# The last two kinds of sums of w_out's blocks issued on GpSimd instead of VectorE, in a kernel of cosine-weighted linear attention and a leaky-ReLU layer

## Chip, cores and metric

The kernel runs on one core of a Trainium2 chip. The metric is the device time of one execution in microseconds; of several executions the median is given. The time before is 271.71 us, the median of three runs (271.64 to 272.72). Beside these one execution was profiled: it took 272.88 us, and the span of its trace, from the first to the last instruction, is 271.0 us.

## The reference

Attention without a softmax over 8 batches, 8 heads, 576 positions and 64 columns per head, and behind it a layer of 512 to 2048 to 512 over the 4608 tokens:

```python
def phi(x, c, s):                      # c, s: cos and sin of pi/2 * position / 576
    r = np.maximum(x, 0.0)
    return np.concatenate([r * c, r * s], axis=-1)
q_p, k_p = phi(q, cos_w, sin_w), phi(k, cos_w, sin_w)
kv = np.einsum('bhsf,bhsd->bhfd', k_p, v)
z = np.sum(k_p, axis=2)
num = np.einsum('bhsf,bhfd->bhsd', q_p, kv)
den = np.einsum('bhsf,bhf->bhs', q_p, z)[..., None] + 1e-06
x = (num / den), heads side by side     # (4608, 512)
h = x @ w_in                            # w_in: 512 x 2048
out = np.maximum(0.01 * h, h) @ w_out   # w_out: 2048 x 512
```

## The kernel before

**Tiles and stages.** The tokens go through in nine groups of 512: groups 0 to 7 are the first 512 positions of each batch, group 8 the 64 last positions of all batches. For each batch the kernel makes `kpm` and `kpt` (phi of k, `k_part`, L268, through `phi_half`, L240 on VectorE and L238 on ScalarE), casts v into `vmain` and `vtail`, multiplies them (`kv_mm`, L291 and L298) and copies the result out as `kv`. For each group it makes `qp` (phi of q), transposes it, multiplies by `kv` (`num`, L375, or in the first two groups `num_half`, L411) and divides (`divide`: `den` L386, `rden` L390, `xs` or `xp` L391, all on VectorE). The quotient is transposed into `xT`, and the two products of the layer follow.

**The two products.** Group 0 uses plain products (`ffn1`, L454; `ffn2`, L470). From group 1 on in the second product, and from group 2 on in the first, a product of 2 x 2 blocks is made with seven block products instead of eight (`p1`, L777; `p2`, L882). This needs sums of the blocks of each operand. The blocks of w_out lie in `w2` (16 chunks of 128 rows, 512 columns): b11 and b12 are the left and right halves of chunks 0 to 7, b21 and b22 those of chunks 8 to 15. `w2_sums(i, s)` makes the sum of kind s for half i of the chunks (chunks 4i to 4i+3 and 8+4i to 11+4i), each one instruction of 128 x 1024 elements in fp16:

- kind 1: `wb1` = b12 - b11
- kind 2: `wb2` = b22 - `wb1`
- kind 4: `wb4` = b21 - `wb2`
- kind 3: b12 = b22 - b12, written over b12 in `w2`

The block product 7 (of `p2`) reads the new b12, the block product 4 reads `wb4`; both come late in the order 1, 2, 6, 5, 7, 4, 3 of `f2_stream`. The plain product of group 0 reads the old b12.

**What sets the order.** All instructions are recorded by hand in one order, and each engine works through its own in that order; an instruction waits by semaphores for what it reads and for earlier readers of what it overwrites. The first part (groups 0 and 1 up to their quotients) is written out line by line, with small lists of steps woven between matmuls. The rest is a list of pairs of a position and a function (`put`), sorted by position and recorded at the end. A group takes 56 or 58 positions. The sums of w_out stand in two places:

- in the woven list of L668: kinds 1 of both halves, kinds 2 and 4 of the first half (`for i, n in ((0, 1), (1, 1), (0, 2), (0, 4)): at(9, w2_sums, i, n)`);
- in the position list, from the table `W2_AT` (L1051, loop L1077): kind 2 of the second half at 16.0, kind 3 of the first half at 29.5 and of the second at 18.5, kind 4 of the second half at 75.5. A table entry with one position serves the second half alone.

All of them are made by VectorE through `sub` (L254), which most other sums of blocks go through too (`gs`, `xw`, `wa`).

**GpSimd** (`POOL` in the code) has ten small setup instructions, and then eleven casts (L248): parts of w_in (`cast_w1`) and of v (`v_main(b, lo, hi, POOL)`, L570, L571 and L678). The last of these, for the second four heads of batch 1, is recorded right behind the four pairs `k_main(1, j, ACT, DVE, 4, 8)` (L677), whose cosine parts are ScalarE's and whose sine parts are VectorE's; `kv_half(1, 1, "n")` (L688) multiplies these.

Of the kernel before, what the change touches and what calls it, by code (L numbers as in the profile page):

```python
# [11 lines left out]
ALU = mybir.AluOpType  # L12
# [6 lines left out]
def kernel(  # L19
# [14 lines left out]
    nc = tc.nc  # L34
# [45 lines left out]
    ACT, DVE, POOL = nc.scalar, nc.vector, nc.gpsimd  # L80
# [169 lines left out]
    def add(o, a, b):  # L250
        nc.vector.tensor_tensor(out=o, in0=a, in1=b, op=ALU.add)  # L251

    def sub(o, a, b):
        nc.vector.tensor_tensor(out=o, in0=a, in1=b, op=ALU.subtract)  # L254

    def kp_tiles(b):
        st["kpm", b] = kppool.tile([P, H, J, F], dt.float16, name="kpm")
# [259 lines left out]

    wb = {s: const.tile([P, NH, N2], dt.float16, name=f"wb{s}") for s in (1, 2, 4)}

    def w2_sums(i, s):  # L520
        lo, hi = slice(4 * i, 4 * i + 4), slice(8 + 4 * i, 12 + 4 * i)
        left, right = slice(0, N2), slice(N2, DM)
        b11, b12 = w2[:, lo, left], w2[:, lo, right]
        b21, b22 = w2[:, hi, left], w2[:, hi, right]
        if s == 1:
            sub(wb[1][:, lo], b12, b11)
        elif s == 2:
            sub(wb[2][:, lo], b22, wb[1][:, lo])
        elif s == 4:
            sub(wb[4][:, lo], b21, wb[2][:, lo])  # L530
        else:
            sub(b12, b22, b12)

    def w1_sums(i, s, lo=0, hi=4):
        a11, a12, a21, a22, s1, s2, s4 = (
# [132 lines left out]
    for i, n in ((0, 1), (1, 1), (0, 2), (0, 4)):  # L668
        at(9, w2_sums, i, n)
# [340 lines left out]
    def put(pos, f, *args):  # L1010
        line.append((pos, len(line), f, args))
# [64 lines left out]
        put(top[ALL - 1] + at_, w1_sums, 1, s, 2, 4)  # L1076
    for s, at_ in W2_AT.items():  # L1077
        for i in range(2 - len(at_), 2):
            put(at_[i - 2], w2_sums, i, s)
    for s, at_ in G1_AT.items():  # L1080
        for u in range(2):
            put(at_[u], g_sums, 1, s, 4 * u, 4 * u + 4)
# [6 lines left out]
    for b in range(2, NG):  # L1089
        at_, eng, s0 = AT[min(b, 5)], ENG[min(b, 5)], top[b] if b > 3 else 0  # L1090
# [53 lines left out]
```

## Time and profile before

| | |
|---|---|
| median of three runs | 271.71 us |
| the profiled execution | 272.88 us |
| its span | 271.0 us |
| mean granted TensorE clock | 0.999 |
| VectorE, all subtractions of L254 of 128x1024 fp16, one instruction | 0.68 us |
| GpSimd, last instruction but for the end of the program | 45.75 to 46.79 us |

The engines are PE (TensorE), PEld (its weight loads), DVE (VectorE), ACT (ScalarE), POOL (GpSimd) and SP (SyncE, which issues the DMAs). The first part of the page gives each engine's busy time, its share of the span and its instructions. The part headed by the chain gives the work that ended last, followed back from the last instruction, in shares of the span. A timeline row has the start in us from the start of the span, the duration in us, the engine, the line of the kernel, the operation, the tile written, an arrow and the tiles read, the shape and the count of merged instructions; in brackets stands how long the engine sat idle before it and what ended that. A row of the chain has start, length and what ran.

### The profile page before, as it was taken

To read this page: it belongs to the slowest core of one execution; us is meant where nothing else is said; L and a number is where in the kernel's file an instruction comes from. 1 tells how busy PE (TensorE), PEld (TensorE's weight loads), DVE (VectorE), ACT (ScalarE), POOL (GpSimd) and SP (SyncE) were. 2 spreads that over 40 slices of the span, in tenths; PEclk is the share of its full clock that TensorE was granted. 3 is DMA by queue.
4 is the path that set the end of the run, shared out by engine and by line. 5 is a ranking of instruction groups with operands and counts; after the bars stand their busy time and mean duration, and the time that the engine had idled before them with its cause. 6 is when DMAs were issued, how large, how long until landed. Compare 5 with 4: busy or idle time off the path is not lost.

```text
span 271.0 us, 6597 instructions
## 1 busy us (share of the span) xinstructions
PE 263.2 (97%) x2660; PEld 226.1 (83%) x2660; DVE 201.6 (74%) x445; ACT 200.8 (74%) x330; POOL 10.6 (4%) x21
## 2 busy tenths in 40 slices
PE   7799999999999999999999999999999999999994
PEld 5786455765888989889999999999999889999983
DVE  5774799797986797899779696979577758644652
ACT  6666556696878998798899789978966756766621
POOL 1055101000000000000000000000000000000000
PEclk9999999999999999999999999999999999999999
DMA  6999999998999869998999699969384412200324
GB/s 229 313 355 409 408 350 371 354 241 269 296 225 350 148 189 259 297 189 238 280 261 158 184 273 271 175 208 157 77 135 160 62 41 95 82 0 2 144 50 119
DMA packets 87150, 57.05 MB, mean 211 GB/s; under 512 B 56656, under 2 KB 82256, under 8 KB 86608
## 3 DMA queue, kind: packets, MB, share of 16 engines
q1 hardware_dynamic: 86816, 56.37, 78.8%
q8 instruction: 21, 0.34, 0.5%
q10 hardware_dynamic: 304, 0.26, 0.3%
q14 instruction: 9, 0.07, 0.1%
HBM read 36.70 MB, written 9.44 MB: 170 GB/s over the span
## 4 chain that ended last, share of the span: by engine, by line
PE 89%; DVE 4%; DMA 3%; ACT 3%; issue 1%; SPq 0%; DVEq 0%; ACTq 0%
PE ps_o L882 33%; PE ps_h L777 29%; PE ps_h L454 5%; PE ps_h L490 5%; PE ps_o L470 5%; PE ps_h L882 3%; PE ps_num L375 3%; DMA kst<-in_k_dram 3%; PE ps_kv L291 2%; ACT g L751 1%; DVE kpm L240 1%; DVE xp L391 1%; PE ps_qt L365 1%; PE ps_kvh L291 1%; PE ps_numh L411 1%
## 5 line engine op out<-in xcount | busy, mean ns | idle before, releaser
L882 PEld LDWEIGHTS <-g 128*128 128x128 f16 x640 | 62.5, 98 | 7.3 <-DVE g L251 0.2
L251 DVE TENSOR_TENSOR u<-ps_h,u 128x512 f32<-128x512 f32 x52 | 35.8, 688 | 25.2 <-PE ps_h L777 22.3
L882 PE MATMUL ps_o<-w,g 128*128 128x256 f16 x352 | 51.2, 273 | 0.0
L777 PEld LDWEIGHTS <-w 128*128 128x128 f16 x416 | 44.4, 114 | 1.2
L777 PE MATMUL ps_h<-xT,w 128*128 128x256 f16 x288 | 43.3, 273 | 0.0
L804 ACT ACTIVATE g<-u 128x1024 f16<-128x1024 f32 x26 | 27.5, 1057 | 10.9 <-DVE u L251 10.8
L777 PEld LDWEIGHTS <-wa 128*128 128x128 f16 x312 | 34.0, 113 | 1.7 <-DVE xw L254 0.6
L790 ACT ACTIVATE g<-ps_h 128x512 f16<-128x512 f32 x52 | 31.2, 602 | 5.7 <-PE ps_h L777 5.7
L797 ACT COPY u<-ps_h 128x512 f32<-128x512 f32 x52 | 30.4, 585 | 5.5 <-PE ps_h L777 5.4
L882 PE MATMUL ps_o<-wb,g 128*128 128x256 f16 x232 | 33.5, 273 | 0.0
L777 PE MATMUL ps_h<-xw,wa 128*128 128x256 f16 x208 | 31.3, 273 | 0.3 <-DVE xw L254 0.3
L882 PEld LDWEIGHTS <-gs 128*128 128x128 f16 x256 | 24.9, 98 | 2.9
L900 ACT COPY ob<-ps_o 128x512 f32<-128x512 f32 (+1 forms) x32 | 17.9, 561 | 9.2 <-PE ps_o L882 9.0
L490 PE MATMUL ps_h<-xT,w 128*128 128x512 f16 (+1 forms) x104 | 24.7, 363 | 0.0
L391 DVE TENSOR_TENSOR xs<-ps_num,rden 128x512 f16<-128x512 f32 x28 | 19.3, 691 | 1.0
L882 PE MATMUL ps_o<-w,gs 128*128 128x256 f16 x120 | 17.8, 273 | 0.0
L251 DVE TENSOR_TENSOR ob<-ps_o,ob 128x512 f32<-128x512 f32 (+1 forms) x22 | 14.8, 674 | 3.7 <-ACT ob L900 1.4
L254 DVE TENSOR_TENSOR gs<-g 128x1024 f16<-128x1024 f16 x16 | 11.0, 688 | 8.8 <-ACT g L804 8.7
L882 PE MATMUL ps_o<-wb,gs 128*128 128x256 f16 x120 | 17.5, 273 | 0.0
L787 ACT COPY ps_h<-ps_h 128x512 f32<-128x512 f32 x26 | 14.9, 572 | 2.3 <-PE ps_h L777 1.5
L777 PE MATMUL ps_h<-xT,wa 128*128 128x256 f16 x104 | 15.6, 273 | 0.0
L777 PE MATMUL ps_h<-xw,w 128*128 128x256 f16 x104 | 15.6, 273 | 0.0
(112 smaller groups left out, 412.3 us busy)
## 6 DMA issues: line engine op xcount, KB each, us to landing
qst<-in_q_dram SPq DMA_DIRECT2D x7, 1024.0 KB, 6.3
out_dram<-ob SPq DMA_DIRECT2D x14, 512.0 KB, 2.8
kst<-in_k_dram SPq DMA_DIRECT2D x6, 1024.0 KB, 8.0
vst<-in_v_dram SPq DMA_DIRECT2D x6, 1024.0 KB, 7.5
w1st<-in_moe_w_in_dram SPq DMA_DIRECT2D x8, 512.0 KB, 9.9
w2st<-in_moe_w_out_dram SPq DMA_DIRECT2D x4, 1024.0 KB, 13.4
kst<-in_k_dram SPq DMA_DIRECT2D x4, 512.0 KB, 7.5
vst<-in_v_dram SPq DMA_DIRECT2D x4, 512.0 KB, 7.9
```

What stands on the lines that cost most here:

```text
L251: nc.vector.tensor_tensor(out=o, in0=a, in1=b, op=ALU.add)
L391: nc.vector.tensor_tensor(out=xs, in0=ps[:, :, 0 : 4 * NE].rearrange("p a (b e) -> p a b e", e=NE)[:, :, :, 0:D], in1=rden.rearrange("p (a ...
L454: nc.tensor.matmul(ps[:, m % 2, lo:hi], lhsT=w1[m // 4][c // 2][:, c % 2, m % 4 : 512 : 4], rhs=xT[:, c, lo:hi], start=(c == 0 and lo == 0 ...
L470: nc.tensor.matmul(ps, lhsT=st["g", g][:, m, tt * P : (tt + 1) * P], rhs=w2[:, m, :], start=(m == 0), stop=(m == NFT - 1),)
L490: nc.tensor.matmul(ps[:, lo:hi], lhsT=w1[m // 4][c // 2][:, c % 2, m % 4 : 512 : 4], rhs=st["xT", g][:, c, lo:hi], start=(c == 0 and lo == 0),
L777: nc.tensor.matmul(bank[:, p], lhsT=w(c), rhs=st["xb", g][n][:, c], start=(fresh and p == 0 and c == 0), stop=(c == 1), skip_group_check=True,
L787: nc.scalar.copy(bank1[bj], bank1[bi])
L790: nc.scalar.activation(st["g" + nm, g][:, 2 * t : 2 * t + 2], bank1[bi], AF.Lrelu)
L797: nc.scalar.copy(st["u", g, t][:, n], bank1[bi])
L804: nc.scalar.activation(st["gt", g][:, :, 1, 2 * t : 2 * t + 2], st["u", g, t], AF.Lrelu)
L882: nc.tensor.matmul(bank, lhsT=st[G2[n], g][:, m, pair * P : (pair + 1) * P], rhs=W2[n](m), start=(fresh and m == 0), stop=(m == NH - 1), s ...
L900: nc.scalar.copy(o_at(g, half_, col, pair), bank_of(bi, pair, pair is None))
```

## The change

`sub` and `w2_sums` get an engine as their last argument, VectorE unless another is given. Kinds 3 and 4 hand it on. The loop over the position table gives GpSimd for kinds above 2. The woven list gives none.

```diff
-    def sub(o, a, b):
-        nc.vector.tensor_tensor(out=o, in0=a, in1=b, op=ALU.subtract)
+    def sub(o, a, b, eng=DVE):
+        eng.tensor_tensor(out=o, in0=a, in1=b, op=ALU.subtract)
...
-    def w2_sums(i, s):
+    def w2_sums(i, s, eng=DVE):
...
         elif s == 4:
-            sub(wb[4][:, lo], b21, wb[2][:, lo])
+            sub(wb[4][:, lo], b21, wb[2][:, lo], eng)
         else:
-            sub(b12, b22, b12)
+            sub(b12, b22, b12, eng)
...
     for s, at_ in W2_AT.items():
         for i in range(2 - len(at_), 2):
-            put(at_[i - 2], w2_sums, i, s)
+            put(at_[i - 2], w2_sums, i, s, POOL if s > 2 else DVE)
```

In the built program GpSimd has three instructions more and VectorE three fewer; the order on TensorE, ScalarE and SyncE is as before.

## The prediction

> **What bounds the kernel now.** I read the busy shares first, then the chain of waits around the places of the moved work, then the timelines of GpSimd (POOL) and VectorE (DVE) there.
>
> ```profile
> PE 263.2 (97%) x2660; PEld 226.1 (83%) x2660; DVE 201.6 (74%) x445; ACT 200.8 (74%) x330; POOL 10.6 (4%) x21
> ...
> PE 89%; DVE 4%; DMA 3%; ACT 3%; issue 1%; SPq 0%; DVEq 0%; ACTq 0%
> ```
>
> TensorE is busy 97% of the span and is 89% of the chain that ends last. So freed VectorE time is worth something only where TensorE waits for VectorE, and any new wait of TensorE is paid in full, since there is almost no idle time later to earn it back in.
>
> The chain (start, length, what) where GpSimd finishes its last work of before:
>
> ```profile
> 47.92 0.45 PE ps_x L428 x8
> 48.37 0.35 PE ps_kvh L291 x8
> 48.72 0.06 PE ps_kvh L298
> 48.77 0.26 PE ps_kvh L291 x8
> ...
> 50.68 0.70 DVE xp L391
> 51.38 0.05 issue
> 51.43 0.40 PE ps_xth L428 x4
> ```
>
> The second group of eight L291 matmuls takes 0.26 us, the first 0.35. The first is paced by its weights, the four `kpm` sine parts that VectorE makes just then. The chain runs on through the sums of L411, the division (L391) and the transposes (L428): all of this is serial.
>
> VectorE and GpSimd there (start, duration, operation, idle before):
>
> ```profile
> 45.75 1.04 POOL L248 CAST vmain<-vst 128x1024 f16<-128x1024 f32 x1 [17.72 <-DMA vst<-in_v_dram]
> ```
>
> ```profile
> 46.59 0.69 DVE L391 TENSOR_TENSOR xp<-ps_numh,rden 128x512 f16<-128x512 f32 x1
> 47.20 1.13 DVE L240 TENSOR_SCALAR kpm<-kst,sin_t 128x256 f16<-128x256 f32 x4
> 48.25 0.68 DVE L248 COPY osb<-ps_o 128x512 f32<-128x512 f32 x1
> ```
>
> The last `kpm` part ends at 47.20 + 1.13 = 48.33, just when TensorE wants it. GpSimd is free from 45.75 + 1.04 = 46.79 to the end.
>
> **The change, part by part.** *What moves.* Three instructions, not four: the position table has kind 3 for both halves (29.5 and 18.5) and kind 4 for the second half only (75.5). Kind 4 of the first half comes from the earlier list (L668), which passes no engine, and stays on VectorE. VectorE loses the two `w<-w` and the last `wb<-w,wb`; GpSimd gets the same three behind its `vmain` cast. No DMA and no matmul moves, and no queue but these two changes its order.
>
> *What VectorE gains.* Each is 0.68 us long and 0.60 from its start to the next one's:
>
> ```profile
> 60.87 0.68 DVE L254 TENSOR_TENSOR w<-w 128x1024 f16<-128x1024 f16 x1
> 61.62 0.17 DVE L386 TENSOR_SCALAR den<-ps_num 128x8 f32<-128x8 f32 x1
> ...
> 88.41 0.17 DVE L386 TENSOR_SCALAR den<-ps_num 128x8 f32<-128x8 f32 x1 [0.48 <-PE ps_num L375]
> ```
>
> That is 3 x 0.60 = 1.8 us of VectorE, but none on the path. The one at 60.87 stands before a `den` at 61.62 that needs the matmuls of L375, and these end at 61.59 in the chain. The one at 68.64 lies in a queue that next goes idle at 79.67 (0.68 us idle, waiting for ScalarE) with TensorE busy throughout. The one at 85.62 is followed by 0.48 us of waiting for TensorE at 88.41. I cost the gain at 0; the most it could be is the 0.45 us that TensorE waits for `xs` at 62.89 and the 0.28 us for `xw` at 97.6, together 0.7.
>
> *When GpSimd starts.* "The same places" holds for the order of recording only. GpSimd does nothing between, so each instruction starts when its own inputs are there. In the built order the first `w<-w` (second half) waits for the casts of w_out (VectorE's ends at 44.70, ScalarE's at 45.32) and for the L470 matmuls that read these rows (over by 43.2, when the first L291 matmuls of this batch stand behind them); the next one has no wait at all. So both start not at 60.87 and 68.64 but back to back at 46.8, right behind the `vmain` cast and across the four `kpm` parts. Kind 4 needs the `wb` of kind 2 (59.66 to 60.34) and starts behind that. Readers are far off: the first product with the new `w` is at 77.47, that with the second half of the last `wb` at 88.65. So no reader waits.
>
> *What GpSimd takes (T each).* No row shows it subtracting. Its casts take 0.61 us for 512 elements and 1.04 for 1024, 0.84 ns for each further element with one input. Lower bound: as the cast, 1.04. Upper: a whole cast for each of the two inputs, 2.08. I take the upper, 2.1, since its row rate per input is the nearest thing; twice 1.04 would be too much only if the two inputs came in at once.
>
> *What it does to VectorE.* One place shows the two engines at once:
>
> ```profile
> 24.99 0.69 DVE L251 TENSOR_TENSOR wa<-w,w 128x1024 f16<-128x1024 f16 x1 [3.15 <-POOL w L248]
> 25.72 1.41 DVE L254 TENSOR_TENSOR wa<-wa,w 128x1024 f16<-128x1024 f16 x1
> 27.16 1.41 DVE L254 TENSOR_TENSOR wa<-w,wa 128x1024 f16<-128x1024 f16 x1
> ```
>
> ```profile
> 25.26 2.77 POOL L248 CAST w<-w1st 128x1024 f16<-128x1024 f32 x2 [0.30 <-DMA w1st<-in_moe_w_in_dram]
> ...
> 26.57 1.46 POOL L248 CAST w<-w1st 128x1024 f16<-128x1024 f32 x1
> ```
>
> Alone the sum takes 0.69 and the cast 1.04; here 1.41 and 1.31 to 1.46. The ends fit strict turns: cast 1 lets go at 26.57, the sum ends 0.56 later (27.13); cast 2 then needs 0.90 more (28.03), the next sum ends 0.54 after that (28.57). Each waits for a whole instruction of the other. Not everything waits: the division `xp` at 46.59, whose large input comes from PSUM, takes its usual 0.69 beside the cast of 45.75, and so does the one at 14.73 beside a cast.
>
> The four `kpm` parts read and write SBUF, with one tensor as input. No row shows such an operation beside GpSimd. Their rate (343 ns at 256 elements, 478 at 512: 0.53 ns each) is that of the sums from SBUF (418 at 512, 682 at 1024: 0.52) and twice that of the sums out of PSUM (422 at 256, 688 at 512: 1.04). So they are nearer to what waits than to what doesn't, and I take it that they wait their turn. Bounds: no effect (0), or full turns. By turns: the first subtraction holds from 46.80 to 48.90; the first `kpm` part ends 0.22 later (its 0.34 less the 0.12 that the blocked sum had done beforehand), the second subtraction follows from about 48.98 to 51.08, the second part ends at 51.30, the third and fourth 0.26 apart at 51.83. That is 51.83 - 48.33 = **3.5 us** late (2T - 0.7). TensorE stands for it at the first L291 group, and all behind it goes late by as much: the copy of `kv`, L411, the division, ScalarE's xT copies and the g evictions queued behind these. The loads into the stage buffers that these parts free go late by as much too.
>
> The Trainium skill, page "SBUF — State Buffer", section "Who interferes with whom", says that GpSimd and VectorE share one pair of ports under an exclusive lock, held for a whole instruction, and that copies, casts and tensor_scalar in a two-port mode fall under it as well as operations with two SBUF inputs; by this rule the sum is the 3.5 us above, and were only the second kind blocked, 0. The turns at 25 us agree for two inputs; no run here shows the other yet. The same skill's "GPSIMD Engine Reference", section 3.1, has 4497 ns for a two-input add of 2048 fp32 elements; half of it, 2.25 us, would be an estimate for T and make the sum 3.8 us, 275.5 in all.
>
> *Kind 4.* When it becomes ready `gs2<-g,gs3` (60.26, two SBUF inputs) is already under way, so GpSimd waits, and then VectorE has three divisions out of PSUM until 66.4. I cost it at 0; if it came first it would hold the `gs2` sum up by T, 2.1, of which the slot of 0.60 given free at 60.87 takes a part: at most 1.5.
>
> *Sum.* 0 + 3.5 + 0. The profiled execution took 272.88 us with a span of 271.0, so 1.9 lies around the span; its span would become 274.5 and its time 276.4. The median of the runs shown is 271.71, 1.17 below that execution, so I forecast 271.71 + 3.5 = **275.2 us**.
>
> **The rivals.**
> 1. *TensorE's clock falls in the stall.* At the end of this trace the granted clock is 1.00 until 270.0 and 0.50 from 270.5, some 2.9 us after the last matmul (267.4). The stall is 3.5 us, with one matmul or two of 65 columns in it. Against: 1.5 us without matmuls at 11 us left the clock at 1.00, and the longest piece here is about 2.1. If it falls, some 3 us of matmuls go at half speed, of which the stretch from 52.9 to 58.8 hides a part (36 matmuls of 0.11 us in 6 us): +1.3, so 276.5. The Trainium skill, "TensorE: Matmul & The Clock Gate", Part 1, gives an idle window of 3413 ns that runs freely of the kernel; the 2.9 us here is in accord.
> 2. *VectorE keeps its turn over all four parts*, as they are issued 0.26 apart without a wait between them (the two sums at 25 us have one). Then only one subtraction is in the way: 46.80 + 2.1 + 0.22 + 3 x 0.26 = 49.9, 1.6 late: 273.3.
> 3. *No wait for one-input operations* (not slower). If the `kpm` parts run beside GpSimd as the division does, nothing on the path is touched, the whole change is hidden and VectorE has 1.8 us more: 271.7, at best 0.7 less, 271.0. It decides by the `kpm` rows: if they still last 0.34 each, this is it.
> 4. *The change moves nothing* is excluded: the built order has the three on GpSimd.
>
> **How the numbers follow.** Full turns with the clock kept 0.52 (T 0.3 us to either side gives 2.9 to 4.1: 274.6 to 275.8), with the clock lost 0.18 (276.5, up to 277.2), one turn 0.16 (273.3), no wait 0.14. The last splits into no change 0.10 and faster 0.04. A difference under 0.5% (1.4 us) can't be told from none here; one turn gives 1.6, so 0.04 of its 0.16 falls within. So faster 0.04, same 0.14, slower 0.82. The range 272.9 to 277.0 leaves out "no wait" and the far end of the lost clock, some 0.18.
>
> **What would show it.** Right: GpSimd's two `w<-w` at about 46.8 to 51.1, near 2.1 us each; the four `kpm` parts from 47.2 lasting over 4 us instead of 1.13; TensorE idle before L291 from about 48.4, released by `kpm`; everything behind it 3.5 us later, and the third subtraction without effect. Wrong: `kpm` at 0.34 each; T near 1; or a subtraction that starts only after 52, in which case the place of the cost would be among the qp and kpm parts there.

## The result, and the profile after

| | before | changed |
|---|---|---|
| median | 272.45 us (6 runs, 271.64 to 273.67) | 277.49 us (6 runs, 275.17 to 278.65) |
| ratio | | 1.0159, 95% interval 1.0125 to 1.0193 |
| span of the profiled execution | 271.0 us | 276.0 us |
| its mean granted TensorE clock | 0.999 | 0.994 |

The changed kernel is slower by some 4.3 us by the ratio, 5.0 us by the two profiled spans. The busy shares and the chain of the changed kernel:

```profile
PE 266.4 (97%) x2660; PEld 227.6 (82%) x2660; DVE 203.5 (74%) x442; ACT 200.8 (73%) x330; POOL 17.3 (6%) x24
...
PE 86%; DVE 6%; DMA 3%; ACT 3%; issue 1%; SPq 0%; DVEq 0%; ACTq 0%
```

GpSimd has three instructions and 6.7 us more. VectorE has three instructions fewer and is busy 1.9 us longer, not 2 us less: it spends the time in waits that count as part of its instructions. Its share of the chain goes from 4% to 6%.

GpSimd's timeline of the changed kernel (start, duration, operation, idle before):

```profile
46.11 1.04 POOL L248 CAST vmain<-vst 128x1024 f16<-128x1024 f32 x1 [17.70 <-DMA vst<-in_v_dram]
47.12 4.25 POOL L254 TENSOR_TENSOR w<-w 128x1024 f16<-128x1024 f16 x2
65.35 2.51 POOL L254 TENSOR_TENSOR wb<-w,wb 128x1024 f16<-128x1024 f16 x1 [13.98 <-DVE wb L254]
```

The two subtractions of kind 3 start right behind the `vmain` cast, 4.25 / 2 = 2.1 us each. VectorE's timeline beside them:

```profile
46.98 0.69 DVE L391 TENSOR_TENSOR xp<-ps_numh,rden 128x512 f16<-128x512 f32 x1
47.59 4.45 DVE L240 TENSOR_SCALAR kpm<-kst,sin_t 128x256 f16<-128x256 f32 x4
...
55.23 0.17 DVE L386 TENSOR_SCALAR den<-ps_numh 128x8 f32<-128x8 f32 x1 [2.59 <-PE ps_numh L411]
```

The four `kpm` parts take 4.45 us instead of 1.13. The division at 46.98, which the first subtraction overlaps from 47.12 on, keeps its 0.69. TensorE's timeline at the same time:

```profile
49.54 0.19 PE L291 MATMUL ps_kvh<-vmain,kpm 128*128 128x65 f16 x1 [0.78 <-DVE kpm L240]
51.57 0.98 PE L291 MATMUL ps_kvh<-vmain,kpm 128*128 128x65 f16 x7 [1.85 <-DVE kpm L240]
...
53.01 1.91 PE L470 MATMUL ps_o<-w,g 128*128 128x512 f16 x4
```

Before, TensorE's row of L470 and VectorE's row of the `den` behind it were

```profile
48.92 1.03 PE L470 MATMUL ps_o<-w,g 128*128 128x512 f16 x4
```

```profile
50.24 0.17 DVE L386 TENSOR_SCALAR den<-ps_numh 128x8 f32<-128x8 f32 x1 [1.32 <-PE ps_numh L411]
```

One matmul comes through after the first `kpm` part, the next one 2.0 us later: that gap is the second subtraction. And the four L470 matmuls take 1.91 us where they took 1.03 before. Why stands in the busy times by stretch (PE, PEld, DVE, ACT and POOL busy, then the granted clock, the DMA share and GB/s):

```profile
50.00:51.00 1.00, 0.00 (x0) 0.00 (x0) 1.00 (x1) 0.00 (x0) 1.00 (x1) 1.00 1.14 349
51.00:52.00 1.00, 0.40 (x2) 0.21 (x2) 1.00 (x4) 0.00 (x0) 0.36 (x1) 0.71 1.08 375
52.00:53.00 1.00, 0.97 (x16) 0.91 (x16) 0.64 (x2) 0.00 (x0) 0.00 (x0) 0.50 1.10 379
...
54.00:55.00 1.00, 1.00 (x11) 0.45 (x9) 0.00 (x0) 0.04 (x1) 0.00 (x0) 0.58 1.08 398
55.00:56.00 1.00, 1.00 (x19) 0.63 (x15) 0.70 (x3) 0.55 (x1) 0.00 (x0) 1.00 0.60 229
```

At the end of the wait the clock falls to half, from about 51.4 to 54.8, and what TensorE has to do in that time runs at half speed.

The 5.0 us of the two spans can be read off one row, the `den` behind L411, at 50.24 before and at 55.23 after, 4.99 later. The `kpm` parts start 0.39 later already (47.59 against 47.20; this start differs from execution to execution, ahead of any changed instruction). They take 4.45 - 1.13 = 3.32 longer. From their end to the `den` it takes 55.23 - 52.04 = 3.19 instead of 50.24 - 48.33 = 1.91, 1.28 more, at half the clock. 0.39 + 3.32 + 1.28 = 4.99, of which 4.6 is the change's. Behind that row everything runs as before, only later.

### The profile page after: what moved, and what is told of

Its sections match the earlier page's. It is cut to its first block, busy times and chain, and to the rows that moved or that the text cites. A ratio compares the mean times of both kernels' runs of the same rounds, so it can differ in the third digit from the quotient of the medians.

```text
span 276.0 us, 6598 instructions
## 1 busy us (share of the span) xinstructions
PE 266.4 (97%) x2660; PEld 227.6 (82%) x2660; DVE 203.5 (74%) x442; ACT 200.8 (73%) x330; POOL 17.3 (6%) x24
## 4 chain that ended last, share of the span: by engine, by line
PE 86%; DVE 6%; DMA 3%; ACT 3%; issue 1%; SPq 0%; DVEq 0%; ACTq 0%
PE ps_o L882 32%; PE ps_h L777 28%; PE ps_h L454 5%; PE ps_h L490 5%; PE ps_o L470 4%; PE ps_h L882 3%; PE ps_num L375 3%; DMA kst<-in_k_dram 3%; DVE kpm L240 2%; PE ps_kv L291 2%; DVE xp L391 1%; ACT g L751 1%; PE ps_kvh L291 1%; PE ps_qt L365 1%; PE ps_xth L428 1%
## 5 line engine op out<-in xcount | busy, mean ns | idle before, releaser
L490 PE MATMUL ps_h<-xT,w 128*128 128x512 f16 (+1 forms) x104 | 24.7, 363 | 0.0
L240 DVE TENSOR_SCALAR kpm<-kst,sin_t 128x512 f16<-128x512 f32 (+1 forms) x34 | 17.3, 522 | 0.0
L470 PE MATMUL ps_o<-w,g 128*128 128x512 f16 x64 | 16.0, 395 | 0.0
```

The source lines that it names most:

```text
L240: eng.tensor_scalar(out=o, in0=i, scalar1=0.0, scalar2=col, op0=ALU.max, op1=ALU.mult)
L470: nc.tensor.matmul(ps, lhsT=st["g", g][:, m, tt * P : (tt + 1) * P], rhs=w2[:, m, :], start=(m == 0), stop=(m == NFT - 1),)
L490: nc.tensor.matmul(ps[:, lo:hi], lhsT=w1[m // 4][c // 2][:, c % 2, m % 4 : 512 : 4], rhs=st["xT", g][:, c, lo:hi], start=(c == 0 and lo == 0),
```

## The experiments

**The same three subtractions at another place.** Kind 4 is recorded ahead of the two of kind 3, so that GpSimd's queue stands until `wb2` is there.

```diff
-    W2_AT = {2: (16.0,), 3: (29.5, 18.5), 4: (75.5,)}
+    W2_AT = {2: (16.0,), 3: (29.5, 18.5), 4: (17.0,)}
```

> The same three subtractions on GpSimd, but kind 4 (which needs wb2, ready at about 60.3 us) is recorded ahead of the two of kind 3, so all three start behind it. My theory (the two engines take turns instruction by instruction; only VectorE operations with both ends in SBUF wait; the place decides): they run at about 61 to 68 us beside divisions out of PSUM, the four kpm parts last 1.13 us again, TensorE does not stand at L291, the clock stays at 1.00; ratio to before 1.000 to 1.002 (at most 0.5 us, for the g sum behind the third division). Rival (three subtractions of 2.1 to 2.5 us on GpSimd cost what they cost wherever they lie, by slowing VectorE or the reads of w2): about 3 us, ratio 1.011 or more.

Measured: 1.0013 (0.9987 to 1.0040). GpSimd's and VectorE's timelines of this kernel:

```profile
59.97 2.44 POOL L254 TENSOR_TENSOR wb<-w,wb 128x1024 f16<-128x1024 f16 x1 [13.97 <-DVE wb L254]
62.36 4.21 POOL L254 TENSOR_TENSOR w<-w 128x1024 f16<-128x1024 f16 x2
```

```profile
46.73 1.13 DVE L240 TENSOR_SCALAR kpm<-kst,sin_t 128x256 f16<-128x256 f32 x4
...
63.08 0.20 DVE L390 RECIPROCAL rden<-den 128x8 f32<-128x8 f32 x1
...
65.30 0.69 DVE L391 TENSOR_TENSOR xs<-ps_num,rden 128x512 f16<-128x512 f32 x1
65.91 1.21 DVE L251 TENSOR_TENSOR g<-g 128x1024 f16<-128x1024 f16 x1
```

The same work on the same engine, and the loss is gone. The divisions beside it keep 0.69, and the small `rden`, which reads and writes SBUF alone, keeps its 0.20. The one sum with two inputs in SBUF that meets the end of the last subtraction takes 1.21 instead of 0.68, where TensorE doesn't wait for it. So it is neither GpSimd's length nor its reads of `w2` that cost, but what stands beside it.

**Kind 4 alone on GpSimd.** The two of kind 3 stay on VectorE (`POOL if s > 3`).

> Only the last subtraction (kind 4 of the second half) on GpSimd, the two of kind 3 back on VectorE. My theory: it waits for wb2, comes behind gs2 and lies beside divisions out of PSUM: no effect, ratio 0.999 to 1.001, kpm parts 1.13 us. Rival (GpSimd's longer time is paid at its reader or on VectorE): over 1 us, ratio 1.004 or more.

Measured: 1.0092 (1.0065 to 1.0118): my expectation failed. GpSimd's, VectorE's and TensorE's timelines:

```profile
59.57 2.43 POOL L254 TENSOR_TENSOR wb<-w,wb 128x1024 f16<-128x1024 f16 x1 [14.03 <-DVE wb L254]
```

```profile
59.33 0.69 DVE L254 TENSOR_TENSOR gs<-g,gs 128x1024 f16<-128x1024 f16 x1
59.94 2.61 DVE L254 TENSOR_TENSOR w<-w 128x1024 f16<-128x1024 f16 x1
62.47 0.15 DVE L386 TENSOR_SCALAR den<-ps_num 128x8 f32<-128x8 f32 x1
```

```profile
63.73 0.41 PE L375 MATMUL ps_num<-kv,qpT 128*128 128x65 f16 x8 [2.16 <-DVE xs L391]
```

The same group of matmuls before:

```profile
62.89 0.41 PE L375 MATMUL ps_num<-kv,qpT 128*128 128x65 f16 x8 [0.45 <-DVE xs L391]
```

GpSimd lets `gs2` go first and then holds the next operation. In the first profile of the changed kernel that is the `den` of a division, out of PSUM; here it is `w<-w`, back in its old place with two inputs in SBUF. It takes 2.61 instead of 0.68, 1.93 more, and `den` and `xs`, on the path, are queued behind it: TensorE waits 2.16 instead of 0.45, 1.71 more. The profiled execution kept the clock; of all eight, four have a mean clock of 0.991 to 0.994 and take 275.06 to 276.05 us, the other four 0.998 or more and 273.69 to 274.43. So in half of the executions a fall of the clock seems to come on top of this wait too; none of these was profiled, so its place is not shown. I had carried "kind 4 costs nothing" over from the changed kernel without looking at what comes back to VectorE. The theory stands, but that is an explanation after the fact, so the next run clears that hold away.

**Kind 4 alone, with the way clear.** As the last one, with VectorE's `w<-w` of the second half recorded ahead of kind 2.

```diff
-    W2_AT = {2: (16.0,), 3: (29.5, 18.5), 4: (75.5,)}
+    W2_AT = {2: (16.0,), 3: (29.5, 15.5), 4: (75.5,)}
```

> As with only kind 4 on GpSimd (which came out 2.5 us slower, 1.0092, against what I expected), but VectorE's kind 3 of the second half is recorded ahead of kind 2 instead of behind gs2, so that it no longer stands behind GpSimd's subtraction. My theory now (I had overlooked that this two-input sum, back on VectorE, is the one that has to wait a whole turn, 2.61 us instead of 0.68, and that a den and xs of the path are queued behind it): TensorE's wait for xs at L375 is 0.45 us again instead of 2.16, ratio 1.000 (0.998 to 1.002). Rival (GpSimd's kind 4 costs through its own length or through the divisions beside it): the wait stays, ratio 1.007 or more.

Measured: 0.9985 (0.9961 to 1.0009). VectorE's and TensorE's timelines:

```profile
60.49 0.68 DVE L254 TENSOR_TENSOR gs<-g,gs 128x1024 f16<-128x1024 f16 x1
61.30 0.17 DVE L386 TENSOR_SCALAR den<-ps_num 128x8 f32<-128x8 f32 x1
```

```profile
62.58 0.42 PE L375 MATMUL ps_num<-kv,qpT 128*128 128x65 f16 x8 [0.45 <-DVE xs L391]
```

Nothing is held, TensorE's wait for `xs` is 0.45 us again, and the clock is 0.997 or more in all twelve executions. The position of one instruction on the other engine was the whole 2.5 us.

**One turn instead of two.** Only kind 3 of the second half on GpSimd (`POOL if s == 3 and i == 1`).

> Only kind 3 of the second half on GpSimd, the other two back on VectorE. My theory of whole turns: one subtraction of 2.1 us from about 46.8, the first kpm part ends behind it, the other three follow 0.26 apart: the four end 1.6 us later than before, TensorE's clock stays at 1.00 since it stands still for only 1.5 us: +1.6 us, ratio 1.006. Rival 1 (the two engines share, each at half speed while both work): the four parts need 1.0 us more at most, ratio 1.003. Rival 2 (VectorE waits until GpSimd's queue of ready work is empty, so that it is the second subtraction that made two turns): as whole turns here, told apart by the rows of the changed kernel alone.

Measured: 1.0056 (1.0036 to 1.0076), 1.5 us; whole turns had been put at 1.006, shares at 1.003 at most. In the profiled execution the data of v came early, and GpSimd's and VectorE's timelines are

```profile
45.55 2.12 POOL L254 TENSOR_TENSOR w<-w 128x1024 f16<-128x1024 f16 x1
```

```profile
46.76 1.85 DVE L240 TENSOR_SCALAR kpm<-kst,sin_t 128x256 f16<-128x256 f32 x4
```

The subtraction ends at 45.55 + 2.12 = 47.67 and the four parts 0.94 behind that, at 48.61: a first part of 0.15 to 0.22 and three more at 0.26 each, as worked out for whole turns. The wait is what is left of GpSimd's instruction when `kpm` comes, here 0.91 us (46.76 to 47.67), which makes the four parts 0.72 longer; at half speed each, they could have lost at most half of the 0.91. The two start at times that differ from run to run, so the wait does too. The subtraction's length alone, without a neighbour that it waits for, is 2.12 us.

**The wait without the fall of the clock.** The changed kernel with 26 matmuls on blank data ahead of the L291 group; they are overwritten by that group.

```diff
-    kv_half(1, 1, "n")
+    kv_half(1, 1, "n", 13)
```

> The changed kernel with 26 matmuls on blank data (256 columns, some 2.8 us) on TensorE ahead of the L291 group that waits for the kpm parts; the wait itself stays. My theory (of the loss of some 5 us, 3.3 is the wait and the rest the clock that falls to 0.50 some 3 us into it): the clock is 1.000 in every run and the kernel 3.3 us slower than before, ratio 1.012 (1.011 to 1.014), about 1.3 us faster than the changed kernel in its slower runs. Rival (the clock makes no difference because the matmuls behind it wait for ScalarE anyway, and the loss is all wait): as the changed kernel, ratio 1.016 or more.

Measured: 1.0139 (1.0112 to 1.0166), within my range, but the interval reaches into the rival's. The clock is 0.997 or more in every execution. TensorE's and VectorE's timelines:

```profile
47.40 3.00 PE L166 MATMUL ps_kvh<-blank 128*128 128x256 f16 x26
50.24 0.52 PE L291 MATMUL ps_kvh<-vmain,kpm 128*128 128x65 f16 x8
```

```profile
46.38 3.99 DVE L240 TENSOR_SCALAR kpm<-kst,sin_t 128x256 f16<-128x256 f32 x4
...
52.29 0.17 DVE L386 TENSOR_SCALAR den<-ps_numh 128x8 f32<-128x8 f32 x1 [1.31 <-PE ps_numh L411]
```

The wait is there, 3.99 - 1.13 = 2.86, and from its end (50.37) to `den` it is 1.92 us, as before (1.91), and not 3.19. The interval was too wide to tell the ratio from the changed kernel's, so both were run once more on one chip.

**Both again.**

> The changed kernel once more, beside the one with blank matmuls on the same chip. My theory: the clock falls in most runs (mean 0.99) and the kernel is 4 to 5 us slower than before, ratio 1.015 to 1.018; runs at a clock of 1.000 are about 2 us shorter than the others. Rival (the clock is of no account): runs with and without the fall take the same time, ratio as with blanks, 1.012.

> The changed kernel with the 26 blank matmuls, once more. My theory: clock 0.997 or more in every run, 1 to 2 us faster than the changed kernel on the same chip, ratio to before 1.011 to 1.014. Rival: no difference from the changed kernel.

Measured: the changed kernel 1.0173 (1.0124 to 1.0222), with the blank matmuls 1.0115 (1.0075 to 1.0155), both within the ranges I had given. Here are all executions of the two in both sets, by mean granted clock:

| | clock 0.994 or less | clock 0.997 or more |
|---|---|---|
| changed kernel | 9 runs, 275.89 to 278.65, median 277.88 | 3 runs, 275.02, 275.17, 275.44 |
| with blank matmuls | none | 12 runs, 274.75 to 277.77, median 276.00 |

Where the clock keeps up, in three runs, the changed kernel takes 275.2 in the mean; in most runs it doesn't. The blank matmuls hold the clock in all twelve, and their kernel's other differences are within its own spread. The separate intervals still overlap; the sorting by clock, with the 1.92 us of the rows above, is what shows the second part of the loss. The two groups of the changed kernel lie 2.7 us apart, and the clock accounts for about half of that: 1.28 in the first profile, 1.35 in the second (0.81 between the `kpm` parts and `den`, 0.54 behind it).

In the second profile the clock falls later, at about 51.9, when the matmuls of L291 have been running again for 1.3 us, and is back at about 55.3. Busy times by stretch, as above:

```profile
51.00:52.00 1.00, 0.94 (x18) 0.74 (x18) 0.65 (x2) 0.16 (x1) 0.00 (x0) 0.95 1.13 366
...
55.00:56.00 1.00, 1.00 (x9) 0.54 (x7) 0.96 (x3) 0.07 (x1) 0.00 (x0) 0.84 0.60 227
```

The repeated profile shows a third part that the first one lacks. VectorE's, GpSimd's and TensorE's timelines of the changed kernel, second profile:

```profile
64.26 2.35 DVE L254 TENSOR_TENSOR gs<-g,gs 128x1024 f16<-128x1024 f16 x1 [0.41 <-ACT g L751]
```

```profile
63.93 2.13 POOL L254 TENSOR_TENSOR wb<-w,wb 128x1024 f16<-128x1024 f16 x1 [13.55 <-DVE wb L254]
```

```profile
67.79 0.42 PE L375 MATMUL ps_num<-kv,qpT 128*128 128x65 f16 x8 [1.29 <-DVE xs L391]
```

Here `gs2` waits 0.41 us for ScalarE, GpSimd's kind 4 comes first and `gs2` takes 2.35; TensorE's wait for `xs` is then 1.29 us instead of 0.45. In the first profile `gs2` was ahead by 0.17 us and nothing happened. That ScalarE is late there because of the slow matmuls is likely: its copy of `xT` comes 2.16 us behind `den` (53.77 to 55.93) instead of 1.62 before (50.24 to 51.86), behind four L490 matmuls that took 1.69 us instead of 1.03. It was not tried by an experiment.

## Why the prediction was right, and where not

*What moves, and when it starts:* right. Three instructions, both of kind 3 at the end of the `vmain` cast (forecast 46.8, measured 47.12 and 46.13 in the two profiles), not at the places of VectorE's.

*Freed VectorE time at 0:* right. With the three taken off VectorE and nothing in the way (the reordered kernel) the ratio is 1.0013 (0.9987 to 1.0040), no gain that can be measured.

*T:* right in the number, 2.1 forecast and 2.12 measured. My reason for it, one cast's time for each of the two inputs, was not tested. The estimate of 2.25 from the Trainium skill, "GPSIMD Engine Reference", section 3.1, was 6% high for fp16 operands.

*One-input operations wait for whole turns:* right. The choice by rate held: operations on SBUF that go at twice the rate of the sums out of PSUM are held (`kpm`, `gs`, `w`, `g`), those with their large input in PSUM are not. Rate and place go together in these rows, so which of the two decides is not shown. I had also written that no row showed an operation on SBUF with one input beside GpSimd; `rden` is one, with 8 elements a row, and takes 0.20 us beside a subtraction as it does elsewhere, in the trace before too (14.49, beside the cast of 14.24). So not everything on SBUF is held. The turns came as drawn: one subtraction, one `kpm` part, one subtraction, three parts. 3.5 forecast; 3.32 and 3.15 measured, 2.86 and 3.12 with the blank matmuls ahead. The Trainium skill, "SBUF — State Buffer", section "Who interferes with whom", names the kinds that were held here, tensor_scalar and operations with two inputs in SBUF; the 4.45 us now show it for the form that no run had shown.

*The clock:* the first rival's mechanism was right, its chance and the reason for its price were not. I gave it 0.18 because the piece between the few matmuls would be only 2.1 us, against 2.9 us at the end of the trace and 1.5 harmless ones at the start. The fall came 2.7 us after the last dense matmuls in the first profile (48.76 to 51.42) and 4.0 us after them in the second (47.94 to 51.91), and 9 of 12 runs have a low mean clock. A mean of 0.994 is what one such stretch makes, since half of 3.4 us is 0.6% of 276; where it fell in the runs without a profile is not shown. The pieces without a matmul were only 0.78 and 1.85 us there, 0.61 and 1.84 in the second, so the one matmul of 65 columns between them did not keep the clock; whether it would fall more often without that matmul no run shows. The price of 1.3 us came out (1.28 and 1.35), but by luck, since my reason for it was wrong: nothing of it is hidden under ScalarE's stretch, as the clock is back before; it is 3.4 us at half speed on short serial work. The "some 3 us" of matmuls had no row behind it. The Trainium skill, "TensorE: Matmul & The Clock Gate", Part 1, has a window of 3413 ns that runs freely of the kernel; 3.4 us of half clock in both profiles, and a fall in some runs and not in others, agree.

*Kind 4 at 0:* right in one profile, 0.84 us in the other. It is a race between `gs2` and GpSimd, which I bounded at 1.5 and then dropped from the sum.

*The sum:* 3.5 us forecast, 4.3 measured by the ratio. Put on the 271.71 us from which I forecast, the ratio gives 276.0 where I had 275.2. The median of 277.49 itself lies above the 277.0 at which my range ended; 0.7 of its distance from 275.2 is the kernel before, whose median in that set is 272.45. The term mis-sized is the lost clock, at nothing in the sum and 1.3 us in most runs: a consequence of the wait, not the wait. That the total is off by no more is in part luck, as the wait came out at 2.9 to 3.3 us and made up for some of the clock. The three runs with the full clock give 275.0 to 275.4, close to 275.2, but that is luck as well: they are 2.7 us above the medians before of their sets (272.45 and 272.59), not 3.5.

## What to carry to other kernels

Before work goes to GpSimd, list VectorE's instructions that will run beside it, and sort them by their rate and by where their operands lie: the large ones on SBUF alone, which here ran at twice the rate of those out of PSUM, were held for a whole GpSimd instruction, two microseconds, those out of PSUM were not. The place where an idle engine starts is set by its waits and not by where the code records it, so an early start can land on the worst neighbour; putting another instruction ahead in its queue that waits for the right moment moved 4 us here at no cost. And a wait of TensorE of about two microseconds may have to be charged twice, once for itself and once for the matmuls at half clock behind it: the mean clock was low in nine of twelve runs where TensorE waited 2.6 us in two pieces, in four of eight where it waited 2.2 in one, in none of eleven with one turn in the way, and in one of the 43 runs of the kernel before that stand beside the experiments.

## What the runs showed of the hardware

I had not expected the clock to fall here: 2.7 and 4.0 us after the last dense matmuls in the two profiles, with no piece without a matmul longer than 1.85 us, and the second time after matmuls had run again for 1.3 us. Both times it stayed at half for 3.4 us. Nor had I expected that a lead of 0.17 us decides: whichever of `gs2` and GpSimd's subtraction came first went through whole, and the other stood, `gs2` for 1.7 us.
